# A chunked RWKV-6 layer with mixture of depths: transposes back to tokens over 112 partitions, results in head order, and an earlier place for the gate's row

## The chip, the cores and the metric

The kernel runs on one core of a Trainium2 chip. The metric is the device time of one execution in microseconds (us); lower is better. The time of a kernel is the median of its runs. The profile is one execution, recorded by the hardware profiler; its span is a little shorter than the device time (203.5 us against 205.24 us for the run that was profiled).

Five engines work side by side and wait for each other through semaphores: PE (TensorE, matrix products and transposes), DVE (VectorE), ACT (ScalarE), POOL (GpSimd) and SP (which issues transfers). "PEld" is the loading of PE's stationary operand, which overlaps its products.

## The reference

Two parts follow each other. The first is a linear recurrence for each of 4 batches and 8 heads over 768 tokens with head dimension 48; the second takes its result as rows of 8 x 48 = 384 numbers, picks the best 128 tokens of each batch by a score, and passes those through a small feed-forward net.

```python
def _attn_ref(r, k, v, w, u):                # r, k, v, w: (4, 8, 768, 48), u: (8, 48)
    for t in range(S):
        kt, vt, rt, wt = k[:, :, t], v[:, :, t], r[:, :, t], w[:, :, t]
        cur = np.einsum('bhd,bhe->bhde', u[None] * kt, vt)
        y[:, :, t] = np.einsum('bhd,bhde->bhe', rt, state + cur)
        state = wt[:, :, :, None] * state + np.einsum('bhd,bhe->bhde', kt, vt)

def _moe_ref(x, w_gate, w1, w2, capacity):   # x: (4, 768, 384); w1: (384, 1024); capacity 128
    scores = np.einsum('bsd,d->bs', x, w_gate)
    out = x.copy()
    for b in range(B):
        top_idx = np.argpartition(-scores[b], capacity)[:capacity]
        xe = x[b, top_idx]
        ye = np.maximum(xe @ w1, 0.0) @ w2
        g = 1.0 / (1.0 + np.exp(-scores[b, top_idx]))
        out[b, top_idx] = x[b, top_idx] + g[:, None] * ye
```

## The kernel before

The 768 tokens of a batch are cut into 6 chunks of L = 128; with 4 batches there are N = 24 chunks, numbered n. A chunk is loaded with its tokens in the partitions. PE transposes w, k and r so that two heads (a pair j of HP = 4) share the partitions: head q = 0 in partitions 0 to 47, head q = 1 in 64 to 111. Partitions 48 to 63 and 112 to 127 are padding (DP = 64 places for D = 48 values). DVE makes running products of the decays ("scans", from the left and from the right), K and R are k and r scaled by these, and the chunk's results are products of R, K and v under a mask. K and the results yt then have to go back to tokens in partitions: these are the transposes that the change is about.

```python
    def spread(to, row):                       # a row of 384 numbers into all partitions
        ps = psM.tile([L, C], FP32, tag="m", name="ps_b")
        nc.tensor.matmul(ps, one_row, row, start=True, stop=True)
        nc.scalar.copy(out=to, in_=ps)

    def transposed(pool, tag, src):
        ps = pool.tile([L, HP, L], FP32, tag=tag, name=f"ps_{tag}")
        for j in range(HP - 1, -1, -1):
            nc.tensor.transpose(ps[:, j, :], src(j), ident)
        return ps
    # ... (cut)
    def back(t):                               # K back to tokens, for the state
        if chunks[t["n"]][1] == NCH - 1:
            return
        ps = transposed(psT, "t", lambda j: t["K"][:, j, :])
        t["kt"] = lev.tile([L, HP, 2, DP], FP32, tag="kt", name="kt")
        nc.scalar.copy(out=t["kt"].rearrange("p j q d -> p j (q d)"), in_=ps)
    # ... (cut)
    def rows_out(t, soon=False):               # the results back to tokens, and out
        b, ci = chunks[t["n"]]
        ps = transposed(psY, "y", lambda j: t["yt"][:, j % 2, j // 2, :])
        y = ps.rearrange("p (a o) (c d) -> p o a c d", o=2, d=DP)
        x = t["x"] = lev.tile([L, C], FP32, tag="x", name="x", bufs=3)
        xh = x.rearrange("p (a o q d) -> p o a q d", o=2, q=2, d=D)
        vo = t.pop("vo")
        for o in (0, 1):
            to = xh[:, o, :, ::-1, :] if o else xh[:, o]
            if soon:
                vh = vo.rearrange("p (a o q) d -> p o a q d", o=2, q=2)
                nc.vector.tensor_add(
                    to, y[:, o, :, :, 0:D], vh[:, o, :, ::-1, :] if o else vh[:, o]
                )
            else:
                nc.scalar.copy(out=to, in_=y[:, o, :, :, 0:D])
        if not soon:
            nc.gpsimd.tensor_add(x, x, vo.rearrange("p h d -> p (h d)"))
        nc.sync.dma_start(out=views[b][b, ci * L:(ci + 1) * L, :], in_=x)
```

In a pair with odd j the two heads of yt are crossed (head 1 lies in the lower half), which is why `rows_out` copies even and odd pairs apart. A turn i works on several chunks at once, in this fixed order:

```python
    def turn(i):
        soon = i >= N - 1
        step(first_left, i + 1)
        if i < 1:
            step(scaled_aside, i + 1, "K", "right")   # K by way of ScalarE and GpSimd
        step(own_products, i + 1)
        step(scores, i)                               # ps_s
        step(own_values, i)
        step(carry, i - 1, work.get(i))
        # ... (cut: K of the next chunk on VectorE, comparisons of scores)
        if not soon:
            step(masked, i)                           # sc
        step(back, i)
        if i == 0:
            warm(2)                                   # matmuls of zeros, to keep PE busy
            spread(wg_bc, wg_row)
        mix(place="half")
        step(rows_out, i - 1, soon)
        step(row_scores_soon if soon else row_products, i - 1)   # uses wg_bc
        step(own_results, i)
        fed_in_turn(PIECES // 2, 2 if i >= N - 1 else 1)         # pieces of the feed-forward net
        step(inputs_t, i + 1, "R", r_bufs)            # transposes of r
        step(scaled, i + 1, "R", "left")
        step(decays_t, i + 2)                         # transposes of w: ps_w
        mix(place="mid")
        if i == -2:
            warm(1)
        step(range_check, i + 2)
        if i == -1:
            spread(u_bc.rearrange("p h d -> p (h d)"), u_row)
            step(own_weights, i + 1)
        step(outputs_t, i)                            # ps_yt, then yt
        step(carry_products, i)                       # ps_kv
        # ... (cut: more pieces of the net)
        step(inputs_t, i + 2, "K", k_bufs)            # transposes of k
        # ... (cut)
        step(scans, i + 2)
        # ... (cut: loads for later chunks)
```

Of the kernel before, what the change touches and what calls it, by code (L numbers as in the profile page):

```python
# [10 lines left out]
FP32 = mybir.dt.float32  # L11
# [7 lines left out]
L = 128  # L19
DP = 64  # L20
# [18 lines left out]
def kernel(  # L39
# [40 lines left out]
    nc = tc.nc  # L80
    PSUM = bass.MemoryType.PSUM

    B, H, S, D = r.shape
# [4 lines left out]
    HP = H // 2  # L88
    NDC = C // L
    NFC = F // L  # L90
    NHF = NCH // 2
    W = HP * L
    assert S % (2 * L) == 0 and C % L == 0 and F % (4 * L) == 0 and H % 2 == 0
    assert HP % 2 == 0 and D <= DP and W <= 512 and C <= 512 and 0 < CAP < S and CAP % L != 1
    assert B * NCH < 256

    consts = ctx.enter_context(tc.tile_pool(name="consts", bufs=1))
    setup = ctx.enter_context(tc.tile_pool(name="setup", bufs=1))
    lev = ctx.enter_context(tc.tile_pool(name="lev", bufs=2))
    mod = ctx.enter_context(tc.tile_pool(name="mod", bufs=1))  # L100
    psW = ctx.enter_context(tc.tile_pool(name="psW", bufs=1, space=PSUM))
    psT = ctx.enter_context(tc.tile_pool(name="psT", bufs=2, space=PSUM))
    psS = ctx.enter_context(tc.tile_pool(name="psS", bufs=1, space=PSUM))
    psY = ctx.enter_context(tc.tile_pool(name="psY", bufs=1, space=PSUM))
# [9 lines left out]
    def crossed(j, q):  # L114
        return q ^ (j & 1)
# [10 lines left out]
    for queue, hs in ((nc.sync, slice(H // 2, H)), (nc.scalar, slice(0, H // 2))):  # L126
        queue.dma_start(
            out=w_bufs[0][:, hs, 0:D], in_=w[0, hs, 0:L, :].rearrange("h t d -> t h d")
# [4 lines left out]
    wg_row = setup.tile([1, C], FP32)  # L133
    nc.scalar.dma_start(out=wg_row, in_=_rows(moe_w_gate, 1))
    u_bc = consts.tile([L, H, D], FP32)
    wg_bc = consts.tile([L, C], FP32)
# [15 lines left out]
    def loads(n):  # L152
        load(v_bufs, v, n - 2)
        load(k_bufs, k, n - 1)
        load(r_bufs, r, n - 1)
        load(w_bufs, w, n)
# [19 lines left out]
    def load_weights(n):  # L176
        while n > 0 and weights:
            to, src = weights.pop(0)
            nc.sync.dma_start(out=to, in_=src)
            n -= 1  # L180


    ident = consts.tile([L, L], FP32)
# [7 lines left out]
    high = consts.tile([L, 1], FP32)  # L191
    nc.vector.memset(high, -HIGH)

    row = setup.tile([L, L], INT32)
    nc.gpsimd.iota(row, pattern=[[1, L]], base=0, channel_multiplier=0)
    slots = consts.tile([L, L], BF16)
# [4 lines left out]
    for t, sign in ((before_f, 1), (after_f, -1)):  # L201
        nc.gpsimd.memset(t, 1.0)
        nc.gpsimd.affine_select(
            out=t, in_=t, pattern=[[sign, L]], base=-1, channel_multiplier=-sign,
# [32 lines left out]
    def warm(n):  # L237

        ps = psM.tile([L, 512], FP32, tag="m", name="ps_n")
        for _ in range(n):  # L240
            nc.tensor.matmul(ps, nothing[:, 0:L], nothing, start=True, stop=True)

    def spread(to, row):
# [8 lines that stand above are left out]
        for j in range(HP - 1, -1, -1):  # L252
            nc.tensor.transpose(ps[:, j, :], src(j), ident)  # L253
        return ps

    def decays_t(t):
        wb = w_bufs[t["n"] % NBUF]
        t["wt"] = transposed(psW, "w", lambda j: wb[:, 2 * j:2 * j + 2, :])

    def scans(t):  # L260
# [5 lines left out]
        nc.vector.tensor_tensor_scan(  # L266
            out=flat[:, W - 2::-1], data0=wt[:, W - 1:0:-1],
            data1=from_right.rearrange("p j t -> p (j t)")[:, W - 2::-1], initial=1.0,
            op0=ALU.mult, op1=ALU.max,
# [7 lines left out]
        nc.vector.tensor_tensor_scan(  # L277
            out=left.rearrange("p j t -> p (j t)")[:, 1:W], data0=wt[:, 0:W - 1],
            data1=start.rearrange("p j t -> p (j t)")[:, 1:W], initial=start[:, 0, 0:1],
            op0=ALU.mult, op1=ALU.max,  # L280
# [6 lines left out]
    def check_sums():  # L287

        above = setup.tile([L, 1], FP32)
        nc.vector.tensor_reduce(out=above, in_=guard, axis=AX.X, op=ALU.add)  # L290
        below = setup.tile([L, 1], FP32)
        junk = setup.tile([L, N * HP], FP32)
        nc.vector.tensor_scalar(
            out=junk, in0=alls.rearrange("p n j -> p (n j)"), scalar1=float(LOW ** L),
            scalar2=None, op0=ALU.is_lt, op1=ALU.add, accum_out=below,
        )
        return above, below
# [20 lines left out]
    def inputs_t(t, name, bufs):  # L318
        src = bufs[t["n"] % NBUF]
        t[name + "t"] = transposed(psT, "t", lambda j: src[:, 2 * j:2 * j + 2, :])  # L320
# [52 lines left out]
    def back(t):  # L373
        if chunks[t["n"]][1] == NCH - 1:
            return
        ps = transposed(psT, "t", lambda j: t["K"][:, j, :])
        t["kt"] = lev.tile([L, HP, 2, DP], FP32, tag="kt", name="kt")
        nc.scalar.copy(out=t["kt"].rearrange("p j q d -> p j (q d)"), in_=ps)

    state = {}  # L380

# [25 lines left out]

    def rows_out(t, soon=False):
        b, ci = chunks[t["n"]]
        ps = transposed(psY, "y", lambda j: t["yt"][:, j % 2, j // 2, :])  # L410
        y = ps.rearrange("p (a o) (c d) -> p o a c d", o=2, d=DP)
        x = t["x"] = lev.tile([L, C], FP32, tag="x", name="x", bufs=3)
        xh = x.rearrange("p (a o q d) -> p o a q d", o=2, q=2, d=D)
        vo = t.pop("vo")
        for o in (0, 1):
            to = xh[:, o, :, ::-1, :] if o else xh[:, o]
            if soon:
                vh = vo.rearrange("p (a o q) d -> p o a q d", o=2, q=2)
                nc.vector.tensor_add(
                    to, y[:, o, :, :, 0:D], vh[:, o, :, ::-1, :] if o else vh[:, o]  # L420
                )
            else:
                nc.scalar.copy(out=to, in_=y[:, o, :, :, 0:D])  # L423
        if not soon:
            nc.gpsimd.tensor_add(x, x, vo.rearrange("p h d -> p (h d)"))  # L425
        nc.sync.dma_start(out=views[b][b, ci * L:(ci + 1) * L, :], in_=x)

    def row_products(t):
# [211 lines left out]
    def step(f, n, *more):  # L640
        if 0 <= n < N:
            f(work.setdefault(n, dict(n=n)), *more)

    def mix(n=1, place=None):


        while n > 0 and mixing:
            if place is not None and mixing[0][1] not in (None, place):
                return
            try:  # L650
                mixing[0][1] = next(mixing[0][0])
                n -= 1
            except StopIteration:
                mixing.pop(0)
# [16 lines left out]
    def fed_in_turn(n, few):  # L671

        kept = (feed or picked) and (feed or picked)[0][0] == B - 2
        fed(few if kept else n, on=False)
# [6 lines left out]
# [4 lines that stand above are left out]
            step(scaled_aside, i + 1, "K", "right")  # L685
        step(own_products, i + 1)
        step(scores, i)
        step(own_values, i)
        step(carry, i - 1, work.get(i))
        if i > 0:  # L690
            step(scaled, i + 1, "K", "right")
        if i >= 0:
            step(own_weights, i + 1)
        if soon:
            step(masked, i)
        if i == N - 1:
            sums.extend(check_sums())
        if i < N:
            step(compared, i - 2)
        if not soon:  # L700
            step(masked, i)
        step(back, i)
        if i == 0:
            warm(2)
            spread(wg_bc, wg_row)
        mix(place="half")
        step(rows_out, i - 1, soon)
        step(row_scores_soon if soon else row_products, i - 1)
        step(own_results, i)
        fed_in_turn(PIECES // 2, 2 if i >= N - 1 else 1)  # L710
        step(inputs_t, i + 1, "R", r_bufs)
        step(scaled, i + 1, "R", "left")
        step(decays_t, i + 2)
        mix(place="mid")
        if i == -2:
            warm(1)
        step(range_check, i + 2)
        if i == -1:
            spread(u_bc.rearrange("p h d -> p (h d)"), u_row)
            step(own_weights, i + 1)  # L720
        step(outputs_t, i)
        step(carry_products, i)
        fed_in_turn(PIECES - PIECES // 2, 1 if i == N - 1 else 0)
        if i == N - 1:
            step(compared, i - 1)
        step(inputs_t, i + 2, "K", k_bufs)
        if not soon:
            step(row_sums, i - 1)
        step(scans, i + 2)
        if 0 <= i - 2 < N - 1 and chunks[i - 2][1] == NCH - 1:  # L730
            mixing.append([mixture(chunks[i - 2][0]), "end"])
        mix(place="end")
        if i > -2:
            loads(i + 5)
        if i in WEIGHT_TURNS:
            load_weights(1)
# [93 lines left out]
```

## Time and profile before

| | before |
|---|---|
| median of three runs | 205.49 us (205.3 to 209.77) |
| span in the profile | 203.5 us |
| transposes of K back to tokens | 80 instructions, mean 274 ns |
| transposes of yt back to tokens | 96 instructions, mean 274 ns |
| copy of kt, ScalarE | 20 instructions, mean 587 ns |
| copies of x, ScalarE | 44 instructions, mean 332 ns |
| spreading of the gate's row, PE | 2 instructions, 0.91 us at 12.04 us |

How to read the profile: its parts are the busy time of each engine with its share of the span, the chain of work that ended last (followed back from the last instruction to what released it), and groups of instructions by source line, engine, operation and tile, with the busy time, the mean duration of one, and the idle time before them with what ended it. A line of the order of time starts with the start in us and the duration; brackets hold an idle time before it and its releaser. Matmuls are pipelined: a single one lasts 274 ns, but the next starts long before it ends, so what counts is the distance of the starts. L253 is the helper `transposed`; the tile tells which transposes are meant (ps_w, ps_t of k_buf, r_buf or K, ps_y).

### The profile page before, as it was taken

The numbers are of one execution on the slowest core, as the hardware profiler recorded it, in microseconds if no ns is written. First come the engines' busy times: TensorE is split into PE (matmuls) and PEld (weight loads), VectorE is DVE, ScalarE is ACT, GpSimd is POOL, SyncE is SP. The second block draws the span as 40 slices with busy tenths as digits, with TensorE's granted clock in tenths as the row PEclk, the third lists the DMA queues.
The fourth block names the chain that finished last, engine by engine and source line by source line (L and its number), as shares of the span: only waits on it lengthen the run. The fifth ranks groups of instructions, "written<-read, shape, count | busy, mean of one in ns | idle before, by whom it ended". The sixth has DMA issues, their size and how long they took to land.

```text
span 203.5 us, 6413 instructions
## 1 busy us (share of the span) xinstructions
PE 190.5 (94%) x2288; PEld 154.9 (76%) x2289; DVE 161.4 (79%) x357; ACT 124.2 (61%) x642; POOL 135.5 (67%) x167
## 2 busy tenths in 40 slices
PE   6799999989899899999999999999999999999980
PEld 2478888868687788898887888898887888876940
DVE  7979999999999968988879788988879884961010
ACT  4487877768854866878354866878355866510300
POOL 6496898886857996678538898669538898111201
PEclk9999999999999999999999999999999999999998
DMA  7999999999999999798792994998872221111101
GB/s 115 163 163 150 178 192 198 243 210 213 205 216 212 259 230 208 142 244 152 137 158 68 169 183 101 151 162 150 122 116 75 46 79 39 41 42 42 39 8 43
DMA packets 105387, 28.81 MB, mean 142 GB/s; under 512 B 100482, under 2 KB 104580, under 8 KB 105348
## 3 DMA queue, kind: packets, MB, share of 16 engines
q1 hardware_dynamic: 104304, 26.65, 75.1%
q0 software_dynamic: 512, 1.57, 2.5%
q8 instruction: 20, 0.33, 0.8%
q14 instruction: 19, 0.16, 0.3%
q10 hardware_dynamic: 532, 0.10, 0.2%
HBM read 22.81 MB, written 5.51 MB: 139 GB/s over the span
## 4 chain that ended last, share of the span: by engine, by line
PE 85%; DVE 4%; DMA 3%; ACT 2%; POOL 2%; issue 2%; SPq 1%; POOLq 0%; DVEq 0%; ACTq 0%
PE ps_t L253 14%; PE ps_s L360 12%; PE ps_h L606 11%; PE ps_f L618 11%; PE ps_yt L393 11%; PE ps_w L253 5%; PE ps_yt L401 5%; PE ps_y L253 5%; PE ps_kv L455 5%; PE ps_e L496 3%; DMA w_buf<-in_w_dram 3%; PE ps_r L522 1%; PE ps_b L246 1%; ACT rk L345 1%; PE ps_x L570 1%
## 5 line engine op out<-in xcount | busy, mean ns | idle before, releaser
L345 ACT ACTIVATE rk<-rk 128x48 f32<-128x48 f32 x192 | 43.6, 230 | 0.1
L425 POOL TENSOR_TENSOR x<-x,vo 128x384 f32<-128x384 f32 x22 | 22.1, 1004 | 22.5 <-ACT x L423 22.4
L345 ACT ACTIVATION_READ_ACCUMULATOR rk<-rk 128x1 f32 x192 | 36.1, 188 | 0.0
L277 DVE TENSOR_TENSOR_SCAN left<-ps_w,from_left 128x511 f32<-128x511 f32 x24 | 30.7, 1281 | 0.9
L406 ACT COPY yt<-ps_yt 128x512 f32<-128x512 f32 x24 | 14.0, 585 | 28.0 <-PE ps_yt L401 25.2
L368 DVE TENSOR_TENSOR sc<-ps_s,before_f 128x1024 f32<-128x1024 f32 x24 | 29.3, 1219 | 0.8 <-PE ps_s L360 0.8
L266 DVE TENSOR_TENSOR_SCAN right_buf<-ps_w,from_right 128x511 f32<-128x511 f32 x24 | 29.1, 1212 | 0.8 <-PE ps_w L253 0.8
L360 PE MATMUL ps_s<-R,K 48*128 48x128 f32 x384 | 27.9, 285 | 0.3 <-ACT yt L406 0.2
L393 PE MATMUL ps_yt<-sc,v_buf 128*64 128x128 f32 x384 | 26.3, 278 | 1.4 <-PE ps_w L253 1.2
L360 PEld LDWEIGHTS ps_s<-R,K 48*128 48x128 f32 x384 | 23.3, 187 | 3.9 <-issue 2.9
L606 PE MATMUL ps_h<-xeT,w 128*128 128x128 f32 x192 | 25.5, 280 | 0.2 <-ACT hid L611 0.2
L336 POOL TENSOR_TENSOR rk<-r_buf,k_buf 128x384 f32<-128x384 f32 x24 | 24.1, 1006 | 1.3 <-DMA r_buf<-in_r_dram 1.2
L393 PEld LDWEIGHTS ps_yt<-sc,v_buf 128*64 128x64 f32 x384 | 20.6, 136 | 5.7 <-issue 2.9
L339 POOL TENSOR_TENSOR rk<-rk,u_bc 128x384 f32<-128x384 f32 x24 | 24.1, 1003 | 1.3 <-DVE alls L272 0.6
L606 PEld LDWEIGHTS ps_h<-xeT,w 128*128 128x128 f32 x192 | 22.9, 192 | 1.6 <-ACT xeT L572 0.5
L618 PE MATMUL ps_f<-w,hid 128*128 128x384 f32 x64 | 23.8, 499 | 0.0
L430 POOL TENSOR_TENSOR scr<-x,wg_bc 128x384 f32<-128x384 f32 x22 | 22.0, 1001 | 1.7
L351 POOL TENSOR_TENSOR vo<-v_buf,own 128x384 f32<-128x384 f32 x24 | 19.9, 830 | 1.3 <-ACT rk L345 1.3
L324 DVE TENSOR_TENSOR R<-ps_t,left 128x512 f32<-128x512 f32 x24 | 16.5, 687 | 5.0 <-ACT own L584 1.6
L324 DVE TENSOR_TENSOR K<-ps_t,right_buf 128x512 f32<-128x512 f32 x22 | 15.1, 685 | 4.9 <-PE ps_t L253 4.9
L253 PE MATMUL ps_w<-ident,w_buf 128*128 128x128 f32 x96 | 15.0, 278 | 1.5 <-ACT every L507 0.7
L313 ACT ACTIVATE junk<-w_buf,high 128x384 f32<-128x384 f32 x24 | 15.1, 630 | 1.0 <-DMA w_buf<-in_w_dram 0.7
(110 smaller groups left out, 348.1 us busy)
## 6 DMA issues: line engine op xcount, KB each, us to landing
k_buf<-in_k_dram SPq DMA_DIRECT2D x24, 192.0 KB, 4.2
r_buf<-in_r_dram SPq DMA_DIRECT2D x24, 192.0 KB, 4.7
v_buf<-in_v_dram SPq DMA_DIRECT2D x24, 192.0 KB, 4.9
out_dram<-x SPq DMA_DIRECT2D x24, 192.0 KB, 3.5
w_buf<-in_w_dram SPq DMA_DIRECT2D x23, 192.0 KB, 5.0
w<-in_moe_w_dram SPq DMA_DIRECT2D x3, 512.0 KB, 6.0
w<-in_moe_w_dram SPq DMA_DIRECT2D x4, 384.0 KB, 4.8
w_buf<-in_w_dram ACTq DMA_DIRECT2D x1, 96.0 KB
```

The source lines that it names most:

```text
L253: nc.tensor.transpose(ps[:, j, :], src(j), ident)
L266: nc.vector.tensor_tensor_scan(out=flat[:, W - 2::-1], data0=wt[:, W - 1:0:-1], data1=from_right.rearrange("p j t -> p (j t)")[:, W - 2::- ...
L277: nc.vector.tensor_tensor_scan(out=left.rearrange("p j t -> p (j t)")[:, 1:W], data0=wt[:, 0:W - 1], data1=start.rearrange("p j t -> p (j ...
L324: nc.vector.tensor_mul(out, t.pop(name + "t"), t.pop(by))
L336: nc.gpsimd.tensor_mul(rk, r_bufs[n % NBUF][:, :, 0:D], k_bufs[n % NBUF][:, :, 0:D])
L339: nc.gpsimd.tensor_mul(t["rk"], t["rk"], u_bc)
L345: nc.scalar.activation(out=rk[:, h, :], in_=rk[:, h, :], func=AF.Copy, accum_out=o[:, h:h + 1])
L360: nc.tensor.matmul(ps[:, q, j, :], t["K"][rows, j, :], t["R"][rows, j, :], start=True, stop=True,)
L368: nc.vector.tensor_mul(t["sc"].rearrange("p q j t -> p (q j) t"), ps.rearrange("p q j t -> p (q j) t"), _heads(before_f, 2 * HP),)
L393: nc.tensor.matmul(ps[half(c), j % 2, j // 2, :], vt[:, 2 * j + q, :], t["sc"][:, q, j, :], start=(j < 2), stop=(old is None), skip_group_ ...
L606: nc.tensor.matmul(ps[:, q, :], w1[:, dc, (f0 + q) * L:(f0 + q + 1) * L], xeT[:, dc, :], start=(dc == 0), stop=(dc == NDC - 1),)
L618: nc.tensor.matmul(ps, hid[:, fc, :], w2[:, fc, :], start=(fc == 0), stop=(fc == NFC - 1))
```

## The change

K and yt are non-zero in partitions 0 to 111 alone, and of each 128 transposed values 2 x 48 = 96 are used. The change transposes 112 partitions with a moving operand of 112 columns. This operand is no longer the identity but a reordered one (`turned`): its first 96 columns pick the 48 values of one head and then the 48 of the other, the last 16 the padding between. So the results come out dense, and with the heads of an odd pair in their right order (its variant x = 1), so that one copy (or one sum) writes all of x. The target kt is now one of two fixed buffers whose padding is zeroed once in the setup. Apart from this, the spreading of the gate's row moves from turn 0 to turn -2, behind the transposes of the first decays, and takes the place of a warm-up matmul there; the two warm-up matmuls of turn 0 go.

```diff
+    DE = DP + D
...
+    turned = consts.tile([DE, 2, DE], FP32)
+    for x in (0, 1):
+        for to, src in ((0, DP * x), (D, DP * (1 - x)), (2 * D, D)):
+            n = min(D, DE - to)
+            nc.gpsimd.tensor_copy(out=turned[:, x, to:to + n], in_=ident[0:DE, src:src + n])
+    kt_bufs = [consts.tile([L, HP, 2, DP], FP32, name=f"kt{i}") for i in range(2)]
+    for t in kt_bufs:
+        nc.gpsimd.memset(t[:, :, :, D:DP], 0.0)
...
+    def dense(pool, tag, src, order):
+        ps = pool.tile([L, HP, DE], FP32, tag=tag, name=f"ps_{tag}")
+        for j in range(HP):
+            nc.tensor.transpose(ps[:, j, :], src(j), turned[:, order(j), :])
+        return ps[:, :, 0:2 * D]
...
-        ps = transposed(psT, "t", lambda j: t["K"][:, j, :])
-        t["kt"] = lev.tile([L, HP, 2, DP], FP32, tag="kt", name="kt")
-        nc.scalar.copy(out=t["kt"].rearrange("p j q d -> p j (q d)"), in_=ps)
+        ps = dense(psT, "t", lambda j: t["K"][0:DE, j, :], lambda j: 0)
+        t["kt"] = kt_bufs[t["n"] % 2]
+        nc.scalar.copy(out=t["kt"][:, :, :, 0:D], in_=ps.rearrange("p j (q d) -> p j q d", q=2))
...
-        ps = transposed(psY, "y", lambda j: t["yt"][:, j % 2, j // 2, :])
-        y = ps.rearrange("p (a o) (c d) -> p o a c d", o=2, d=DP)
+        y = dense(psY, "y", lambda j: t["yt"][0:DE, j % 2, j // 2, :], lambda j: crossed(j, 0))
         x = t["x"] = lev.tile([L, C], FP32, tag="x", name="x", bufs=3)
-        (the loop over even and odd pairs, as printed above)
+        xj = x.rearrange("p (j e) -> p j e", j=HP)
+        vo = t.pop("vo").rearrange("p (j q) d -> p j (q d)", q=2)
+        if soon:
+            nc.vector.tensor_add(xj, y, vo)
+        else:
+            nc.scalar.copy(out=xj, in_=y)
+            nc.gpsimd.tensor_add(xj, xj, vo)
         nc.sync.dma_start(out=views[b][b, ci * L:(ci + 1) * L, :], in_=x)
...
         step(back, i)
-        if i == 0:
-            warm(2)
-            spread(wg_bc, wg_row)
         mix(place="half")
...
         step(decays_t, i + 2)
         mix(place="mid")
+        step(range_check, i + 2)
         if i == -2:
-            warm(1)
-        step(range_check, i + 2)
+            spread(wg_bc, wg_row)
         if i == -1:
             spread(u_bc.rearrange("p h d -> p (h d)"), u_row)
```

More of the change, by code (lines that the diff above doesn't have):

```diff
@@ L409, in rows_out @@
         b, ci = chunks[t["n"]]
-        ps = transposed(psY, "y", lambda j: t["yt"][:, j % 2, j // 2, :])
-        y = ps.rearrange("p (a o) (c d) -> p o a c d", o=2, d=DP)
+        y = dense(psY, "y", lambda j: t["yt"][0:DE, j % 2, j // 2, :], lambda j: crossed(j, 0))
         x = t["x"] = lev.tile([L, C], FP32, tag="x", name="x", bufs=3)
[L413 to L425, printed above, removed]
+        xj = x.rearrange("p (j e) -> p j e", j=HP)
[5 more added lines that the diff above has]
+            nc.gpsimd.tensor_add(xj, xj, vo)
         nc.sync.dma_start(out=views[b][b, ci * L:(ci + 1) * L, :], in_=x)
```

## The prediction

> **What bounds the kernel now.** I read the page first, for the busy shares and the chain that ended last:
>
> ```profile
> PE 190.5 (94%) x2288; PEld 154.9 (76%) x2289; DVE 161.4 (79%) x357; ACT 124.2 (61%) x642; POOL 135.5 (67%) x167
> PE 85%; DVE 4%; DMA 3%; ACT 2%; POOL 2%; issue 2%; SPq 1%; POOLq 0%; DVEq 0%; ACTq 0%
> ```
>
> TensorE (PE) is busy for 94% and owns 85% of the chain. That would make every saved matmul nanosecond count, but it is an average, so next I cut the span into three stretches (columns: stretch, length, busy us and instructions of PE, weight load, DVE, ACT, POOL, then clock, DMA share, GB/s):
>
> ```profile
> 14.00:70.00 56.00, 52.78 (x739) 44.07 (x739) 54.82 (x109) 40.88 (x228) 45.10 (x51) 1.00 1.17 207
> 70.00:170.00 100.00, 100.00 (x1256) 84.35 (x1254) 85.06 (x175) 67.16 (x352) 73.30 (x83) 1.00 0.74 139
> 170.00:203.50 33.50, 27.00 (x239) 20.45 (x235) 10.53 (x40) 7.54 (x30) 7.77 (x9) 0.98 0.12 39
> ```
>
> From 14 to 70 us VectorE (DVE) is the full engine: 54.82 of 56 us, and the 1.15 us missing are only the small steps between dependent instructions, the longest 0.10 us. It never waits for PE there. PE looks full only because it fills its time beside it. From 70 to 170 us the expert layers have started: PE is busy 100.00 of 100 us, while DVE has 15 us of idle time. So a shorter PE instruction is worth nothing in the first stretch and all of itself in the second. The third is the end of the expert layers with few transposes in it.
>
> Then the place of the other edit, just before 14 us: DVE in order of time (start, duration), and the chain of the same stretch:
>
> ```profile
> 11.42 1.20 DVE L368 TENSOR_TENSOR sc<-ps_s,before_f 128x1024 f32<-128x1024 f32 x1
> 13.63 0.69 DVE L324 TENSOR_TENSOR R<-ps_t,left 128x512 f32<-128x512 f32 x1 [1.01 <-PE ps_t L253]
> 14.24 1.21 DVE L266 TENSOR_TENSOR_SCAN right_buf<-ps_w,from_right 128x511 f32<-128x511 f32 x1
> ```
> ```profile
> 10.97 1.03 PE ps_t L253 x4
> 12.00 0.04 issue
> 12.04 0.91 PE ps_b L246 x2
> 12.95 0.59 PE ps_t L253 x4
> 13.54 0.44 PE ps_w L253 x4
> ```
>
> DVE stands still for 1.01 us because the transposes of r for chunk 1 sit in PE's queue behind two warm-up matmuls and behind the spreading of the gate's row (ps_b). After that wait DVE runs without a hole for 56 us, so this one wait shifts everything behind it.
>
> **What the Trainium skill says.** "TensorE: Matmul & The Clock Gate", section "LDWEIGHTS (loading the stationary operand)": a weight load costs by its columns, not by the contraction rows. The data is the stationary side here and keeps 128 columns, so 112 rows instead of 128 should not shorten it. No transpose in this trace has other than 128 rows to test this. The section's columns/1.2 would give 107 ns; the trace has these transpose loads faster, since two of 142 ns take 0.20 us together:
>
> ```profile
> 9.22 0.20 PEld L253 LDWEIGHTS ps_t<-ident,k_buf 128*128 128x128 f32 x2 [0.55 <-issue]
> ```
>
> The second starts some 57 ns after the first, so the load is hidden under the previous matmul. The same page, "Back-to-back issue gap", has the gap between matmuls as moving columns over the clock plus 2.5 ns, 56 ns for 128. The chain in a PE-bound turn shows about twice that:
>
> ```profile
> 90.42 0.44 PE ps_t L253 x4
> 90.86 0.44 PE ps_y L253 x4
> ```
>
> 0.44/4 = 109 ns each: my reading is two array cycles for each fp32 column, 107 ns, plus the fixed 2 to 3. What the page says in kind (the gap scales with the moving columns) is then what the saving rests on. "ScalarE: Activation LUTs", section "What ACT_TABLE_LOAD costs", gives a fixed part plus 0.833 ns per element; the groups agree in slope (512 against 384 elements: (585-478)/128 = 0.84 ns):
>
> ```profile
> L406 ACT COPY yt<-ps_yt 128x512 f32<-128x512 f32 x24 | 14.0, 585 | 28.0 <-PE ps_yt L401 25.2
> L423 ACT COPY x<-ps_y 128x192 f32<-128x192 f32 x44 | 12.0, 332 | 0.0
> L378 ACT COPY kt<-ps_t 128x512 f32<-128x512 f32 x20 | 11.7, 587 | 2.2 <-PE ps_t L253 2.2
> L572 ACT COPY xeT<-ps_x 128x384 f32<-128x384 f32 x4 | 1.9, 478 | 6.9 <-PE ps_x L570 6.9
> ```
>
> **The change part by part.**
> 1. The transposes of K (20 chunks x 4 = 80) and of y (24 x 4 = 96) stream 112 columns instead of 128. By the reading above each takes 107 x 112/128 + 2.5 = 96 ns instead of 109.5, a saving of 13.4 ns. All 176 come to 2.36 us of PE time. By where they start: 32 + 36 lie between 14 and 70 us, beside the full DVE, and are worth nothing; 44 + 52 = 96 lie between 70 and 170 us and are worth 96 x 13.4 ns = 1.29 us; 8 lie behind 170 us, partly on the chain, about 0.1 us; 4 lie before 14 us, 0.05 us.
> 2. Gate row. At turn 0 PE loses two warm-up matmuls (about 0.43 us: the piece of 1.03 less the 0.59 that four transposes behind a wait take in the same chain) and the 0.91 us of ps_b. That is 1.3 us of PE time; DVE gets back the 1.01 us that it waited, not more, because then its own mask (11.42 + 1.20 = 12.62) is the last to end. The same 0.91 us come back at turn -2, behind the first decays, where PE stood idle: from the first decays and one warm-up, finished at 4.8 us, to 5.42 us, where k lands. ps_b then runs from about 4.44 to 5.35 us, just before k. The gate's row was issued at 2.03 us; its packet is through at 3.65 us, so it is there. Cost: about 0. ScalarE's copy of 0.47 us moves to a place where ScalarE is waiting for DVE.
> 3. ScalarE: kt's copy goes from 587 to about 478 ns (384 elements), 20 x 0.11 = 2.2 us; two copies of 192, which take 0.52 to 0.56 us together in the timeline, become one of 478 ns, 22 x 0.06 = 1.3 us. ScalarE is at 61%, and where the chain runs through it (67 to 69.5 us) it is behind a gather and two products on GpSimd. Worth 0 to 0.1 us. The two sums on DVE at the end become one each: 0.62 to about 0.55 us, beside PE.
> 4. Added: six small copies and two fills on GpSimd in the setup, 8 x about 0.15 us = 1.2 us. GpSimd finished its setup at 3.84 us and idled for 3.23 us until 7.07 us, so they are hidden. GpSimd's sum of x keeps its 384 elements (1004 ns).
>
> Sum: 1.0 + 1.29 + 0.15 = 2.4 us. I take 0.2 off for what part 2 may lose to loads: the start is fed by transfers that land about 1.2 us apart, and GpSimd already waits for r of chunk 2 until 16.26 us (1.17 us idle, released by a DMA). A start that is 1 us earlier meets the landings of chunk 2 with almost no slack. So 205.5 - 2.2 = 203.3 us.
>
> **Rivals.**
> A. A transpose does not get shorter with fewer moving columns (a fixed cost, or the weight load underneath sets the 109 ns). For it: load and matmul both have 128 columns in every such transpose of this trace, so the trace cannot separate them fully. Against it: the 57 ns between two loads. The time would be about 204.4 us.
> B. The 1 us at turn 0 is eaten by the loads: k, r and w of chunks 2 and 3 land when they land, and DVE gets its hole a turn later. For it: the wait on r of chunk 2. Against it: PE took k of chunk 2 at 15.38 us without a wait, and DVE does not use it before 17.34 us. The time would be about 204.1 us; with A, 205.3.
> C. The spreading at turn -2 delays the first scores: if the gate's row lands late, the transposes of k wait behind it. DVE waits there anyway, and the first scores start only at 9.80 us, so a slip of half a us hides. It would cost up to 0.5 us. The lost warm-ups could also cost clock; PE stays busy through them, and the granted clock is 1.00, so I don't expect it.
> D. In the PE-bound stretch another engine takes over. DVE has about 1 us idle per turn of 7.3 us, and only 0.11 us per turn is taken from PE. Unlikely.
>
> **Range and chances.** The mechanism of part 2 is seen directly as a wait; part 1 rests on an inferred scaling. Rivals A and B set the upper end, 204.7; the lower end, 202.3, has both parts in full and something from ScalarE or from scheduling around 64 to 70 us. Two per cent faster would be 201.4 us, more than the whole sum; two per cent slower, 209.6 us, would need a new stall. So nearly all of the chance is within 2%, with the sign clearly to the faster side.
>
> **What would show it.** Step 1: K's and y's four transposes in 0.38 to 0.39 us instead of 0.44 in the chain. Step 2: the 1.01 us before R at 13.6 us gone, R starting near 12.6 us, and DVE again without holes to about 69 us; ps_b at 4.4 us. Step 3: kt's copy near 478 ns. Wrong if DVE shows a new wait for PE or a DMA between 12 and 25 us, if the first scores start later than 9.9 us, or if PE is no longer full between 69 and 169 us.

## The result, and the profile after

The changed kernel took 206.81 us (four executions, 206.63 to 206.91) against 205.4 us before: 1.0072 of the time, 95% interval 1.0054 to 1.0089. It is slower by 1.4 us where 2.2 us less were predicted, and outside the predicted range. One sentence is needed to read all numbers below: the executions of one kernel fall into groups, because the PE clock rises early and stays up in some of them and rises late or falls again in others, and a ratio leaves out executions more than 1.5% above the fastest of their kernel, so that the groups are given as well.

The shares of the page and of its chain hardly moved:

```profile
PE 193.1 (94%) x2286; PEld 156.7 (76%) x2286; DVE 161.3 (79%) x355; ACT 121.2 (59%) x620; POOL 136.8 (67%) x175
PE 86%; DVE 4%; ACT 2%; POOL 2%; issue 2%; DMA 2%; ACTq 1%; POOLq 0%; DVEq 0%
```

PE is busy 193.1 us instead of 190.5, though it has less to do. The chain of the same PE-bound turn as before shows that the new transposes (ps_t L272 of K, ps_y) are as short as predicted, 0.38 to 0.39 us for four instead of 0.44:

```profile
93.11 0.39 PE ps_t L272 x4
93.50 0.38 PE ps_y L272 x4
```

So are ScalarE's copies (groups of the changed kernel; before 587 ns, and two of 332 ns):

```profile
L436 ACT COPY x<-ps_y 128x384 f32<-128x384 f32 x22 | 10.7, 485 | 0.0
L397 ACT COPY kt<-ps_t 128x384 f32<-128x384 f32 x20 | 9.6, 482 | 2.5 <-PE ps_t L272 2.5
```

The loss lies in the first 17 us. PE in order of time, the changed kernel:

```profile
3.84 1.09 PE L265 MATMUL ps_w<-ident,w_buf 128*128 128x128 f32 x4
5.61 1.61 PE L258 MATMUL ps_b<-wg_row,one_row 1*128 1x384 f32 x2 [0.68 <-DMA wg_row<-in_moe_w_gate_dram]
7.15 1.11 PE L265 MATMUL ps_t<-ident,k_buf 128*128 128x128 f32 x4
9.90 1.64 PE L258 MATMUL ps_b<-u_row,one_row 1*128 1x384 f32 x2
12.52 2.08 PE L379 MATMUL ps_s<-R,K 48*128 48x128 f32 x16
16.19 0.82 PE L265 MATMUL ps_w<-ident,w_buf 128*128 128x128 f32 x4
```

and the same stretch of the kernel before:

```profile
3.87 0.74 PE L253 MATMUL ps_w<-ident,w_buf 128*128 128x128 f32 x4
5.42 0.63 PE L253 MATMUL ps_t<-ident,k_buf 128*128 128x128 f32 x4 [0.60 <-DMA k_buf<-in_k_dram]
8.38 0.91 PE L246 MATMUL ps_b<-u_row,one_row 1*128 1x384 f32 x2
9.80 1.16 PE L360 MATMUL ps_s<-R,K 48*128 48x128 f32 x16
```

Two things are to be seen. The row of the gate came late: PE stood for 0.68 us. And everything takes nearly twice its time: the same sixteen score products 2.08 us instead of 1.16, the same spreading of u 1.64 instead of 0.91, four transposes 1.09 to 1.11 instead of 0.63. Within the line of 16.19 us the pace changes to the usual one. PE runs at half speed until 16.63 us, where the clock's record has its rise; in the profile before that rise is at 3.93 us. (The clock view cannot show it here: its first record in this profile is the rise itself. The distance of the instructions does show it.)

VectorE pays for it, in the changed kernel:

```profile
14.65 1.22 DVE L387 TENSOR_TENSOR sc<-ps_s,before_f 128x1024 f32<-128x1024 f32 x1 [1.62 <-PE ps_s L379]
16.49 0.69 DVE L343 TENSOR_TENSOR R<-ps_t,left 128x512 f32<-128x512 f32 x1 [0.61 <-PE ps_t L265]
```

The first mask starts at 14.65 us, 3.23 us later than the 11.42 before; R of chunk 1 at 16.49 us, 2.86 later than 13.63. From there on the stretches are as they were:

```profile
17.00:72.00 55.00, 51.62 (x736) 42.90 (x735) 53.85 (x108) 38.65 (x215) 43.58 (x50) 1.00 1.12 199
72.00:172.00 100.00, 99.62 (x1262) 83.81 (x1263) 85.93 (x178) 66.01 (x342) 74.47 (x83) 1.00 0.73 140
```

VectorE is full until 72 us and keeps the delay (mask of chunk 8: 64.64 us instead of 61.81, 2.83 later), then PE is full (99.62 of 100 us) and the shorter transposes take some of it back: the last product with the gate (`ye`) starts at 199.19 us instead of 197.46, 1.73 later.

### The profile page after: what moved, and what is told of

The parts are those of the page before. It is cut to its first block, busy times and chain, and to the rows that moved or that the text cites. A ratio compares the mean times of both kernels' runs of the same rounds, so it can differ in the third digit from the quotient of the medians.

```text
span 205.1 us, 6394 instructions
## 1 busy us (share of the span) xinstructions
PE 193.1 (94%) x2286; PEld 156.7 (76%) x2286; DVE 161.3 (79%) x355; ACT 121.2 (59%) x620; POOL 136.8 (67%) x175
## 4 chain that ended last, share of the span: by engine, by line
PE 86%; DVE 4%; ACT 2%; POOL 2%; issue 2%; DMA 2%; ACTq 1%; POOLq 0%; DVEq 0%
PE ps_s L379 12%; PE ps_h L618 11%; PE ps_f L630 11%; PE ps_yt L412 11%; PE ps_t L265 11%; PE ps_w L265 6%; PE ps_yt L420 5%; PE ps_kv L467 5%; PE ps_y L272 4%; PE ps_t L272 4%; PE ps_e L508 3%; DMA wg_row<-in_moe_w_gate_dram 2%; PE ps_b L258 2%; PE ps_r L534 1%; ACT rk L364 1%
## 5 line engine op out<-in xcount | busy, mean ns | idle before, releaser
L379 PE MATMUL ps_s<-R,K 48*128 48x128 f32 x384 | 28.8, 291 | 0.3 <-ACT yt L425 0.2
L379 PEld LDWEIGHTS ps_s<-R,K 48*128 48x128 f32 x384 | 24.1, 193 | 4.0 <-issue 3.0
L265 PE MATMUL ps_w<-ident,w_buf 128*128 128x128 f32 x96 | 16.0, 292 | 1.3 <-ACT every L519 1.0
L265 PE MATMUL ps_t<-ident,k_buf 128*128 128x128 f32 x96 | 15.9, 291 | 0.0
```

The lines of the kernel that those rows point to most:

```text
L379: nc.tensor.matmul(ps[:, q, j, :], t["K"][rows, j, :], t["R"][rows, j, :], start=True, stop=True,)
```

## The experiments

Four theories are tested, and the numbers are used in the expectations below: (1) the dense transposes give what was predicted; the three warm-up matmuls that the change removes are what let the clock rise early, and losing them costs more than the rest gains. Rivals: (2) the dense half is what costs; (3) the change keeps the clock low in every execution; (4) the late row and its place in PE's queue cost.

### The two halves apart

The dense transposes alone (gate row and warm-ups in their old places):

```diff
         step(back, i)
+        if i == 0:
+            warm(2)
+            spread(wg_bc, wg_row)
...
+        if i == -2:
+            warm(1)
         step(range_check, i + 2)
-        if i == -2:
-            spread(wg_bc, wg_row)
```

> The dense transposes alone: gate row and the warm-up matmuls stay where they were. Theory 1 (the dense half of the change is worth its 1.3 to 1.4 us, the move of the gate row costs the rest, by a late row and a half-speed PE clock until 16.6 us): 204.0 us, clock at full speed from 4 to 7 us, K and y transposes 95 ns apart. Theory 2 (the clock of the changed kernel was late by chance of the profile and the dense half is what costs): 206.5 us or more.

Measured: six executions, three at 203.98 to 204.18 us and three at 207.13 to 208.45; ratio 0.989 (0.9699 to 1.0081). The lowest group is 1.1 us below the lowest of before (205.0 to 205.6 beside it). The size fits theory 1, but the second group was in neither theory. The profile is of one of these slower executions (207.39 us): its clock was up at 4.94 us, down at 8.35 and up again at 15.18. So the three warm-ups, which this kernel has, do not always hold the clock either.

The move alone is the reverse edit, the move's lines of the change put into the kernel before.

> The kernel before with the move alone (gate row at turn -2, no warm-ups at turns -2 and 0), transposes as before. Theory 1: 206.8 + 1.4 = 208.2 us, PE at half speed until about 16 us, the spreading waits for the gate row until about 5.5 us. Theory 2: 205.4 us or less, since one wait of 1.0 us is gone.

Measured: 207.25 us, twenty executions spread over groups: four at 204.5 to 204.8, four at 205.5 to 205.7, two at 206.8, ten at 207.7 to 208.3; ratio 1.0011 (0.9989 to 1.0032). The move is thus able to save 0.6 us, and half of its executions lie some 2.7 us above the lowest group of before. But the kernel before is no single number either: of its 41 executions beside these four kernels, 21 lay at 205.0 to 205.6 us and 20 at 208.3 to 211.6. On average the move alone took 206.8 us and the kernel before 207.5, so that the move makes the lowest group rarer, but is not shown to cost anything on average.

### One warm-up matmul back, and another place for the row

The changed kernel with one line back, ahead of the spreading:

```diff
         mix(place="mid")
+        if i == -2:
+            warm(1)
         step(range_check, i + 2)
         if i == -2:
             spread(wg_bc, wg_row)
```

> The changed kernel with the one warm-up matmul of turn -2 kept, ahead of the spreading. If the missing warm-up is what leaves the clock at half speed (theory 1a): full speed from about 6.5 us, and only the wait for the late row is left: about 204 us. If the stall and the long one-row matmuls in that place are the cause (theory 1b): still half speed until 13 us or later, 206.5 us.

Measured: 204.27 us; fifteen of twenty-one executions at 203.4 to 204.8, one at 205.6, five at 206.9 to 207.2; ratio 0.9939 (0.991 to 0.9969). Neither 1a nor 1b holds by itself: a single matmul of 0.4 us turns the odds (7 of the 24 executions of the change itself are at or below 204.8 us), but does not settle them.

The changed kernel with the row at turn 0 behind the transposes of r and w:

```diff
         mix(place="mid")
+        if i == -2:
+            warm(1)
         step(range_check, i + 2)
-        if i == -2:
+        if i == 0:
             spread(wg_bc, wg_row)
```

> The changed kernel with the gate row spread at turn 0 behind the transposes of r and w (where PE waits for the mask anyway), the warm-up of turn -2 kept, those of turn 0 gone. Theory 1: both halves of the gain without the loss: R of chunk 1 no longer waits 1.0 us, 203.0 us. Theory 2: no better than the dense half alone.

Measured: 203.59 us, four executions from 203.32 to 204.84; ratio 0.9875, but with so few an interval of 0.973 to 1.0021.

### The change again, and the row without its wait

The changed kernel was run again, unedited.

> The changed kernel once more, unedited, with more executions. Theory 1 (the PE clock rises early in some executions and near 16 us in others; the change makes the late rise likelier, but its work is shorter): times in groups as the move alone had them (204.5 to 208.3) less the 1.4 us of the dense half: from 203.1 to 206.9 us, most at 206.3 to 206.9. Theory 3 (the change keeps the clock low in every execution): all at 206.6 to 206.9 us, as in its first four.

Measured: 205.82 us, twenty executions: four at 203.4 to 203.6, three at 204.1 to 204.5, four at 205.4 to 206.0, nine at 206.3 to 207.1; ratio 0.9964 (0.9929 to 0.9999). This is theory 1's spread, and theory 3 falls: the first four executions were all of the upper group. With them it is 13 of 24 executions at 206.2 or above. On average these twenty took 205.5 us, and the 42 of before beside them 207.4: by that measure the change is faster. The profile of this run caught the clock going down again (stretches as in the prediction, the clock is the number behind POOL's brackets):

```profile
4.50:7.90 3.40, 2.41 (x14) 1.24 (x12) 2.84 (x4) 2.50 (x10) 1.19 (x5) 1.00 1.52 164
7.90:11.40 3.50, 3.50 (x10) 1.87 (x10) 2.92 (x5) 1.09 (x4) 1.80 (x3) 0.50 1.53 163
11.40:14.80 3.40, 3.40 (x24) 3.07 (x24) 1.78 (x2) 2.70 (x18) 3.18 (x4) 0.50 1.52 163
14.80:18.20 3.40, 3.40 (x29) 3.07 (x29) 2.58 (x6) 0.86 (x4) 3.32 (x4) 0.50 1.51 164
18.20:21.60 3.40, 3.40 (x49) 3.06 (x46) 3.08 (x4) 3.16 (x20) 0.29 (x1) 1.00 1.54 166
```

The clock came up at 4.52 us, fell at 7.93 us and came back at 18.17 us, although PE was busy all the time in between.

The gate's row loaded ahead of u's row, to take the wait away:

```diff
+    wg_row = setup.tile([1, C], FP32)
+    nc.scalar.dma_start(out=wg_row, in_=_rows(moe_w_gate, 1))
     u_row = setup.tile([1, C], FP32)
     nc.scalar.dma_start(out=u_row, in_=_rows(u.rearrange("h d -> (h d)"), 1))
-    wg_row = setup.tile([1, C], FP32)
-    nc.scalar.dma_start(out=wg_row, in_=_rows(moe_w_gate, 1))
```

> The changed kernel with the gate's row loaded ahead of u's row, so that it lands some 0.6 to 1.3 us earlier. If the wait for the late row is the loss (theory 4): no PE idle before ps_b, k's transposes near 5.4 us, 203.3 us in most executions. If what matters is how much full matmul work PE has before 6 us (theory 1): the wait goes, but the clock still rises late in as many executions, best 203.0, most at 206 to 206.5 us.

Measured: 206.79 us, four executions from 206.65 to 206.97; ratio 1.006 (1.0037 to 1.0082). PE in its profile:

```profile
4.86 0.91 PE L258 MATMUL ps_b<-wg_row,one_row 1*128 1x384 f32 x2
5.70 0.66 PE L265 MATMUL ps_t<-ident,k_buf 128*128 128x128 f32 x4
8.02 1.09 PE L265 MATMUL ps_w<-ident,w_buf 128*128 128x128 f32 x4 [0.60 <-DVE left L296]
```

There is no wait before ps_b, k's transposes start 0.3 us after their old place, and still from 8.02 us on four transposes take 1.09 us: half speed. The wait is not what costs (theory 4 falls). How often the clock fails here cannot be told from four executions.

### The clock held up on purpose

Two warm-up matmuls more, where PE waits for loads anyway:

```diff
         step(inputs_t, i + 1, "R", r_bufs)
+        if i == -1:
+            warm(1)
...
         step(inputs_t, i + 2, "K", k_bufs)
+        if i == -2:
+            warm(1)
```

First in the kernel before:

> The kernel before with the same two warm-up matmuls. Its executions are at 205.0 to 205.6 us in half of the cases and at 208.3 to 211.6 us in the others. Theory 1: the upper groups thin out, the lower one stays at 205.2 us. If the groups are not from the clock: no change in their shares.

Measured: 205.23 us, all twenty executions from 205.03 to 205.56; ratio 0.9997 (0.9989 to 1.0005). Of the 42 executions of before beside it, 23 were that low and 19 at 208.5 to 211.4. The upper groups did not thin out, they are gone. The clock goes with them: averaged over an execution, the granted clock was 0.959 to 0.982 in each of the 19 high executions of before, and 0.990 or more in each of the 23 low ones and in all twenty filled ones. So the upper groups come from the clock.

The same two in the changed kernel:

> The changed kernel, the gate row at turn -2 as in the change, with one warm-up matmul behind the first transposes of k and one behind those of r. Theory 1 (the loss is the clock, and the clock needs matmul work in the first 10 us): nearly all executions at 203.3 to 204.0 us. If the place of the row itself costs (late row, longer queue): still several groups up to 207 us.

Measured: 203.59 us, four executions from 203.51 to 203.75; ratio 0.9919 (0.9896 to 0.9941). Its profile still has the late row:

```profile
5.61 0.88 PE L258 MATMUL ps_b<-wg_row,one_row 1*128 1x384 f32 x2 [0.59 <-DMA wg_row<-in_moe_w_gate_dram]
10.07 1.16 PE L379 MATMUL ps_s<-R,K 48*128 48x128 f32 x16
```

The wait of 0.59 us is there and hides; with the clock up the scores start at 10.07 us and take 1.16. Four of the twenty executions of the unfilled change came out as low (203.4 to 203.6 us). So the loss in its first four executions, 206.8 against 203.6, is the clock's. VectorE in the same profile shows the gain of the move:

```profile
12.80 0.68 DVE L343 TENSOR_TENSOR R<-ps_t,left 128x512 f32<-128x512 f32 x1
17.10 1.22 DVE L387 TENSOR_TENSOR sc<-ps_s,before_f 128x1024 f32<-128x1024 f32 x1
```

R no longer waits. In the filled kernel before it waited 1.01 us, and the mask of chunk 1 started later:

```profile
18.14 1.21 DVE L368 TENSOR_TENSOR sc<-ps_s,before_f 128x1024 f32<-128x1024 f32 x1
```

The lead is 1.03 us at this mask and 0.83 at that of chunk 2 (23.10 against 23.93).

And in the dense half alone:

> The dense transposes alone, with the same two warm-up matmuls. With the clock up early in all executions this is the dense half by itself: 205.2 - 1.2 = 204.0 us, in one group.

Measured: 204.15 us (203.8 to 204.35); ratio 0.9942 (0.9919 to 0.9965). Against the filled kernel before, the dense half is worth 205.23 - 204.15 = 1.1 us.

Last, with the row behind the decays of turn 0:

> As the run with the gate row behind the decays of turn 0, with one warm-up matmul more behind the first transposes of k and one behind those of r, where PE waits for loads. Theory 1: the clock rises by 7 us and stays up in nearly all executions; best 203.2 us, median under 203.8 us. If the warm-ups do not hold the clock: groups up to 207 us as before.

Measured: 203.43 us, seven executions from 203.25 to 204.5; ratio 0.9912 (0.9883 to 0.994). This version beats both kernels, on one level with the filled change. Its VectorE:

```profile
12.67 0.68 DVE L343 TENSOR_TENSOR R<-ps_t,left 128x512 f32<-128x512 f32 x1
22.91 0.35 DVE L514 SCALAR_TENSOR_TENSOR ahead<-ps_e,score,after_f 128x128 bf16<-128x128 f32 x1 [0.27 <-PE ps_e L508]
```

The hole before R is gone, and the mask of chunk 1 starts at 16.96 us, against 18.14 in the filled kernel before: 1.17 us earlier (before rounding). At the mask of chunk 2 it is 0.75 us (23.18 against 23.93): VectorE meets a new wait of 0.27 us. PE in the same profile waited for k of chunk 2 (the line below), ran without a wait from there to that ps_e, and took k of chunk 3 at 20.89 us; that load landed at 20.76 us.

```profile
15.07 0.63 PE L265 MATMUL ps_t<-ident,k_buf 128*128 128x128 f32 x4 [0.25 <-DMA k_buf<-in_k_dram]
```

From the mask of chunk 2 to that of chunk 9 (23 to 68 us) the lead stays at 0.74 to 0.75 us, turn for turn. From there it grows to 1.70 us at the mask of chunk 23 and 1.84 at the last `ye`.

### What feeds the clock

The kernel before with the two fills over one partition instead of 128:

```diff
+    def thin(n):
+        ps = psM.tile([L, 512], FP32, tag="m", name="ps_n")
+        for _ in range(n):
+            nc.tensor.matmul(ps, nothing[0:1, 0:L], nothing[0:1, :], start=True, stop=True)
...
+        if i == -1:
+            thin(1)
...
+        if i == -2:
+            thin(1)
```

> The kernel before with two matmuls of the same length as those warm-ups, but over one partition instead of 128 (zeros all the same). If PE's time counts for the clock, as the full ones did: one group at 205.2 us. If the number of rows counts (theory 1 with the one-row spreading worth little): the groups of 208 to 211 us stay in about half of the executions.

Measured: 205.5 us, seven of twelve executions at 205.15 to 205.56 and five at 208.4 to 211.2; ratio 0.9999 (0.9987 to 1.0011). That is the share of the kernel before (53 of its 98 executions were in the low group), while full fills of the same length had twenty of twenty. One row means one row of both operands; which of the two counts was not separated. The one-row matmul lasts as long as a full one,

```profile
5.85 0.39 PE L247 MATMUL ps_n<-nothing 1*128 1x512 bf16 x1
```

so PE's busy time alone does not keep the clock up.

The kernel before without its three warm-ups at turns -2 and 0:

```diff
         if i == 0:
-            warm(2)
             spread(wg_bc, wg_row)
...
-        if i == -2:
-            warm(1)
         step(range_check, i + 2)
```

> The kernel before, the gate row in its old place, without the three warm-up matmuls that the change removes. Theory 1: the lower group falls from half of the executions to a quarter or less; its fastest ones are at 204.8 us, as PE has 0.4 us less to do in front of the transposes of r. If the three warm-ups do not matter: half of the executions below 205.7 us.

Measured: 210.55 us, four executions from 209.41 to 210.78; ratio 1.024 (1.0183 to 1.0297). None of the four is in the low group, so the 204.8 us were not seen. Its clock, in stretches:

```profile
4.50:7.90 3.40, 1.46 (x11) 0.90 (x10) 2.96 (x5) 2.04 (x9) 0.77 (x1) 0.96 1.53 163
7.90:11.40 3.50, 3.50 (x10) 1.86 (x10) 2.81 (x5) 1.14 (x4) 1.67 (x3) 0.50 1.53 163
18.20:21.60 3.40, 3.40 (x38) 3.14 (x38) 3.03 (x5) 1.55 (x11) 0.27 (x1) 0.55 1.53 163
```

Here the spreading of the row is where it always was, so the clock falls without the move of the row as well. That it does so more often without the warm-ups rests on these four executions; 45 of the 98 of the kernel before lay above its low group too.

The lowest and the other groups, together (us):

| kernel | executions | lowest group | others | average of all |
|---|---|---|---|---|
| before, beside the other runs | 98 | 53 at 204.9 to 205.7 | 208.3 to 211.6 | 207.4 |
| before, filled | 20 | 20 at 205.0 to 205.6 | none | 205.2 |
| before, filled with one-row matmuls | 12 | 7 at 205.2 to 205.6 | 208.4 to 211.2 | 207.4 |
| before, fewer warm-ups | 4 | none | 209.4 to 210.8 | 210.3 |
| the move alone | 20 | 4 at 204.5 to 204.8 | 205.5 to 208.3 | 206.8 |
| the change, all executions | 24 | 4 at 203.4 to 203.6 | 204.1 to 207.1, 13 of them from 206.2 | 205.7 |
| the change, one warm-up kept | 21 | 8 at 203.4 to 203.8 | 204.2 to 207.2 | 204.8 |
| the change, filled | 4 | 4 at 203.5 to 203.8 | none | 203.6 |
| dense half, filled | 4 | 4 at 203.8 to 204.4 | none | 204.1 |
| dense, row behind the decays, filled | 7 | 6 at 203.3 to 203.9 | 204.5 | 203.6 |

## Why the prediction was wrong

**The step that failed is in rival C and in part 2.** It said: "The lost warm-ups could also cost clock; PE stays busy through them, and the granted clock is 1.00, so I don't expect it." The sum therefore counted PE at full speed from the start. Both reasons were bad. The 1.00 came from one profile, which had caught an execution with an early rise; 45 of 98 executions of that kernel were some 3 us or more above the others, at a lower clock. And busy is the wrong measure: in the repeated change, between 7.9 and 18.2 us, PE was busy without a gap and still at half speed. One of the prediction's own signs showed it: the first scores were to start by 9.9 us, and they started at 12.52. The filled kernels show it from the other side: with the warm-ups given back in places where they cost nothing, the change takes 203.59 us, and 203.3 was predicted.

**A part of the loss was chance.** The four executions of the result were all late, while three of the four of before beside them were early; of the twenty executions that followed, eleven were below 206 us. Averaged over all executions the change took 205.7 us and the kernel before 207.4: the change has its own lowest group less often (4 of 24 against 53 of 98), but its late executions are less late (at most 3.7 us above its lowest, against 6.7 for before). That losing the warm-ups costs more than the rest gains, as theory 1 had it, is so in the first four executions and not on average. The two profiles, too, differ by more than the edit: up to 4.4 us PE runs the same instructions in both, and yet the clock had risen at 3.93 us in one and not in the other. What removed warm-ups can do is seen better in the repeated change, where the clock rose at 4.52 us and fell one step of 3.41 us later.

**The gate's row.** "its packet is through at 3.65 us, so it is there" took the data's packet for the landing that PE waits for. The landing was signalled at 4.94 us in the profile before and at 5.47 us in the changed kernel, and PE waited 0.68 us for it. The size of the term was wrong, 0 instead of 0.6 to 0.7 us of PE time; rival C's judgement that a slip of half a microsecond hides was right, since the filled change has such a wait (0.59 us) and its first mask starts at 11.69 us, against 11.62 in the filled kernel before.

**Part 1, the dense transposes,** held: 95 ns apart instead of 109.5 (96 predicted), and nothing of it shows while VectorE is full. The sum was 1.29 us and some 0.1; measured 1.1 (filled) and 1.1 between the mask of chunk 8 and the end of the changed kernel (2.83 - 1.73). Why 0.2 to 0.3 us are missing stays open; comparing the filled kernels turn by turn, most turns from chunk 10 on gain about 0.1 us, three only 0.03 to 0.04, and two (from the mask of chunk 11 to that of 12, and from 17 to 18) nothing. Rival A falls, and so does D: PE stays full.

**Part 2, the hole of 1.01 us,** held once the clock was held up: with the row out of the way R follows the mask at once. In the filled change 1.03 us were won at chunk 1 and 0.83 remained one turn later, so that 0.2 was lost, as had been taken off; with the row behind the decays it was 1.17 and 0.75, a loss of 0.42. Rival B was right in kind (PE waited for k of chunk 2 in both), but far from its size of the whole 1 us.

**Part 3 and 4** held: kt's copy 482 ns (478 predicted), no visible gain from ScalarE, and GpSimd's setup work hidden.

So in the executions of the result the sign was lost by one term that was not in the sum: 12.7 us more of PE at half speed (3.93 us before, 16.63 us after, the two rises in the profiles), which set the first mask back by 3.23 us, against a gain of 1.6 us (filled change against filled kernel before) that was really there.

## What to carry to other kernels

Before a warm-up matmul is removed because PE looks busy without it, check the clock: look at the distance of equal instructions at the start (four of these transposes in 0.63 us or in 1.09), in more than one execution, and treat the warm-ups as work with a purpose until a run without them shows the contrary. If the times of a kernel fall into groups some microseconds apart, fill PE's waits at the start with matmuls over all 128 partitions and see if the groups close; here that was two matmuls, cost no time, and took 3 to 6 us from almost half of the executions. Until the groups are closed, judge a change by its groups and its average over many executions: four executions here showed one group alone. And a load is there when its semaphore says so, not when its data packet ends: 1.3 us lay between the two.

## What the runs showed of the hardware

The clock of PE rose and fell in steps of 3.41 us, or multiples of it: in the profile of the repeated change it was up for one such step and down for three (10.24 us), in the kernel before without the three warm-ups down for four (13.65 us). The steps do not start with the kernel (first rises at 3.93, 4.20, 4.52, 4.90 and 5.09 us in five of the profiles), so the same instructions meet them at another place in every execution. The Trainium skill has this, in "TensorE: Matmul & The Clock Gate", section "What's actually happening": a free-running window of 3413 ns and only half or full clock; these runs agree, with 3.41 us and 0.50 or 1.00. Why the times lie in a few fixed groups although the steps lie anywhere was not shown. Not expected was what counts as activity: full matmuls of zeros over 128 rows do (twenty of twenty executions low with two of them more), while matmuls of the same length over one row were worth nothing measurable (seven of twelve low, where 53 of 98 are without them). That the fp32 transposes, the one-row spreadings and the 48-row scores between 8 and 16 us did not bring the clock back while they filled PE's time is seen in every late profile; how much each of them counts was not measured apart.
